# A ring of eight PSUM banks for the seven products, sums on VectorE, and four weight sets converted during the attention

## The chip, the cores and the metric

The kernel runs on one core of a Trainium2 chip. The metric is device time in microseconds (us); for the kernel before it is 731.38 us, the median of three runs (730.93 to 731.45).

## The reference

Attention with a learned relative-position bias, then a layer that takes the maximum of three products:

```python
scores = (q @ k.transpose(0, 1, 3, 2)) / sqrt(64) + bias      # 4 batches, 8 heads, 576 x 576
attn = exp(scores - max); attn = attn / (sum(attn) + 1e-9)
x = (attn @ v).transpose(0, 2, 1, 3).reshape(2304, 512)
h = maximum(maximum(x @ w1, x @ w2), x @ w3)                  # w1, w2, w3: 512 x 768
out = h @ w_out                                               # 768 x 512
```

All of it is float32. The four weight matrices arrive as 8-byte numbers and are turned into float32 by bit operations on the chip.

## The kernel before, in words

The program has four stages. Instructions go to each engine in the order in which the code is written; every engine works its own list in that order, so an instruction that waits holds up all behind it.

1. Bias stage (to about 60 us): VectorE, ScalarE and TensorE make the position bias.
2. Attention (to about 311 us): 80 steps of scores, exponential, normalisation (GpSimd), transposes and the product with v. `step` (L363) writes one step; its argument `more` is a list of generators, each of which is advanced once in the step. One is `first()`: it converts weights. `convert` (L469) loads half a set (512 KB) and makes five VectorE passes (L479, L481, L484, L487, L492) over 512 columns; two such halves are a weight set. In the attention sets 0 and 1 and the six pieces of `w_out` are converted. Another generator, `combine(0)`, makes the operands of the first third of the tokens.
3. Product stage (311 to 643 us): x @ w1, x @ w2, x @ w3 as 9 weight sets (`s`: three matrices for three pairs of hidden blocks) times three token thirds (`x`), 27 groups in all, set after set. A group (`group`, L584) forms a 2 x 2 block product with seven block products p1 to p7 in place of eight; their sums give four results c11, c12, c21, c22, which are kept as maxima in `ht`. One product is six matmuls of 384 columns, since each operand is a high and a low part (hi*h, hi*l, lo*h, over two halves). p1 and p6 share one PSUM tile `p16` of two banks, p5 and p7 another, `p57`; ScalarE copies p1, p5 and p2 to SBUF (L599, L605, L614), VectorE adds four products to SBUF tiles, and GpSimd makes three sums of 384 columns. Between the products the generator `work(s)` is advanced: `load_w` converts set s + 1, `split_w` forms its seven weight combinations (four GpSimd sums `ws`) and splits them into high (`wh`, ScalarE) and low parts (`wl`, GpSimd, 768 and 1024 columns). During set 0 `combine(x + 1)` is advanced instead.
4. Second product (646 to 727 us): `h` went to DRAM (`store`), comes back transposed in blocks (`load_h`, `hin`), is split (`hh`, `hl`) and multiplied with the split `w_out`.

DMAs are issued from one queue (SP), in the order of the code.

Of the kernel before, what the change touches and what calls it, by code (L numbers as in the profile page):

```python
# [9 lines left out]
F32 = mybir.dt.float32  # L10
# [9 lines left out]
def kernel(  # L20
# [31 lines left out]

    def ps_t(name):
        return psums[-1].tile([128, 512], F32, tag="t", bufs=2, name=name)
# [7 lines left out]
    wo_d = dram.tile([DFF, DM], F32, name="wo_d")  # L62
    raws = []
# [124 lines left out]
    class Attention:  # L188
        def __init__(self, pool):
            self.pool = pool  # L190
            self.data = {}
            self.st = {}
            self.et = {}
            self.pvq = []
            self.done = []
            self.vl = [pool.tile([128, 2, D], F32, name=f"vl{x}", bufs=1) for x in range(2)]
            for x in self.vl:
                nc.gpsimd.memset(x, 0.0)
            bias_t.extend(pool.tile([128, 2, S], F32, name=f"bias{t}", bufs=1) for t in range(NTQ))
            bias_t.append(pool.tile([128, S], F32, name="biasm", bufs=1))  # L200
# [268 lines left out]
    def convert(pool, srcs, out, name):  # L469
# [4 lines left out]
        for _ in range(2):  # L474
# [21 lines left out]
    wf = {}  # L496

    def load_w(wpool, s):
        fp, i = divmod(s, 3)
        m = (mw1, mw2, mw3)[i]  # L500
        raw = wpool.tile([128, 1024], F32, tag="wr", bufs=2, name=f"wr{s}")
        wf[s] = raw
        for d in range(2):
# [4 lines left out]
    def split_w(pool, wpool, s):  # L508
# [3 lines left out]
        hi = pool.tile([128, 1792], F32R, tag=f"wh{s % 2}", bufs=1, name=f"wh{s}")  # L512
        lo = pool.tile([128, 1792], F32R, tag=f"wl{s % 2}", bufs=1, name=f"wl{s}")
        wf[s] = (hi, lo)
        g = nc.gpsimd
        arith(g, q(sr, 0), q(raw, 0), q(raw, 2), ALU.add)
        nc.scalar.copy(hi[:, 0:768], raw[:, 256:1024])
# [5 lines left out]
        yield  # L523
        nc.scalar.copy(hi[:, 768:1792], sr)
        arith(g, lo[:, 0:768], raw[:, 256:1024], hi[:, 0:768])
        yield
        arith(g, lo[:, 768:1792], sr, hi[:, 768:1792])
# [5 lines left out]
    def moe(pool, wpool, xa, xb):  # L533
        ht = pool.tile([128, 2, NT], F32, name="ht", bufs=1)
        hv = ht.rearrange("p b (t n) -> p (b t) n", t=2)
# [5 lines left out]
        def load_wo(fs):  # L541
            raw = wpool.tile([128, 1024], F32, tag="wr", bufs=2, name=f"wor{fs[0]}")
            n = len(fs)
            nc.sync.dma_start(out=raw[:, 0:512 * n].rearrange("p (c o) -> p c o", c=n),
                              in_=wo_d[128 * fs[0]:128 * fs[-1] + 128].rearrange("(c p) o -> p c o", p=128))
            if fs[0] % 3 == 0:
                hi, lo = (pool.tile([128, 1536], F32R, tag=f"w{k}{'o' if fs[0] else 1}", bufs=1, name=f"wo{k}{fs[0]}")
                          for k in "hl")
                for x in range(3):
                    wo[fs[0] + x] = (hi[:, 512 * x:512 * x + 512], lo[:, 512 * x:512 * x + 512])  # L550
            for _ in range(3):
                yield
            for x, f in enumerate(fs):
                hi, lo = wo[f]
                src = raw[:, 512 * x:512 * x + 512]
                nc.scalar.copy(hi, src)
                arith(nc.gpsimd, lo, src, hi)
                yield
# [25 lines left out]
        def group(s, x, work):  # L584
            fp, i = divmod(s, 3)
            r = slice(TW * x, TW * x + TW)
            p16, p57 = ps_s(f"p16_{s}_{x}"), ps_s(f"p57_{s}_{x}")
            p1, p6, p5, p7 = (p[:, n, 0:TW] for p in (p16, p57) for n in range(2))
            p2, p4 = (ps_t(f"p{n}_{s}_{x}")[:, 0:TW] for n in (2, 4))
            p3 = psums[-1].tile([128, TW], F32, tag="pv" if x % 2 else "l", bufs=1, name=f"p3_{s}_{x}")  # L590
            m1, m2, m3, mu = (pool.tile([128, TW], F32, tag="m", bufs=4, name=f"m{n}_{s}_{x}") for n in "123u")
            if i:
                mm, mn = (pool.tile([128, 2, TW], F32, tag="mm", bufs=2, name=f"m{n}_{s}_{x}") for n in "mn")
                c21, c22, c11, c12 = (m[:, n] for m in (mm, mn) for n in range(2))
            else:
                c21, c22, c11, c12 = (hv[:, n, r] for n in range(4))
            v, g = nc.vector, nc.gpsimd
            product("p1", p1, s, x)
            nc.scalar.copy(m1, p1)  # L599
            next(work, None)  # L600
            product("p6", p6, s, x)
            arith(v, m2, p6, m1, ALU.add)
            next(work, None)
            product("p5", p5, s, x)
            nc.scalar.copy(mu, p5)  # L605
            next(work, None)
            product("p7", p7, s, x)
            arith(v, m3, p7, m2, ALU.add)
            arith(g, m2, m2, mu, ALU.add)
            arith(g, c22, m3, mu, ALU.add)  # L610
            next(work, None)
# [200 lines left out]
```

## Time and profile before

| | us |
|---|---|
| median of three runs | 731.38 |
| profiled execution | 729.17 |
| its span | 727.4 |
| TensorE busy | 620.4 (85%) |
| VectorE / GpSimd / ScalarE busy | 440.0 / 365.4 / 344.6 |

The profile is of one execution. Its span is what the engines' records cover; the execution's own time is 1.8 us longer. TensorE's busy share is high in all stages but means little by itself: matmuls are pipelined and their ends are modelled. What counts is the distance between the starts of matmuls, and the waits before them.

### The profile page before, as it was taken

Reading aid. Unit: us, or ns where it says so; the run is one execution under the profiler, and the core shown is the slowest. Engines: PE = TensorE matmul, PEld = TensorE weight load, DVE = VectorE, ACT = ScalarE, POOL = GpSimd, SP = SyncE. Lnnn points to the kernel's source line nnn. Section 1 sums busy time; section 2 is a strip of 40 time slices with the busy share of each in tenths; the row PEclk is TensorE's granted clock in tenths of the full one; section 3 lists DMA queues with packets and bytes.
Section 4 is the critical chain, followed back from the end, with each engine's and each line's share of the span. In section 5 each row is a group of like instructions: output and inputs, shape, how many; then the busy total and the mean of one; then the engine's idle time right before and its main releaser. Section 6 shows DMA issues by size and latency. Waiting matters only on the chain.

```text
span 727.4 us, 12064 instructions
## 1 busy us (share of the span) xinstructions
PE 620.4 (85%) x4342; PEld 486.3 (67%) x4342; DVE 440.0 (60%) x899; ACT 344.6 (47%) x794; POOL 365.4 (50%) x339
## 2 busy tenths in 40 slices
PE   8999999999999999977849495858676776879998
PEld 4457777666767667656748484747666765758887
DVE  7986778678868877878365625272825173632221
ACT  8988878887977887644121211111111112222232
POOL 3408666966665664568754525453544447610000
PEclk9999999999999999986999879897979697989999
DMA  6994462245337311110010321010222001365331
GB/s 179 276 341 156 119 192 91 83 146 154 117 98 221 119 60 27 52 43 1 0 59 0 116 72 59 0 59 0 79 81 86 1 29 45 96 210 187 136 126 70
DMA packets 59595, 72.50 MB, mean 100 GB/s; under 512 B 22800, under 2 KB 41616, under 8 KB 59536
## 3 DMA queue, kind: packets, MB, share of 16 engines
q1 hardware_dynamic: 59392, 71.44, 31.0%
q8 instruction: 34, 0.56, 0.3%
q10 hardware_dynamic: 144, 0.29, 0.1%
q14 instruction: 25, 0.20, 0.1%
HBM read 47.46 MB, written 24.26 MB: 99 GB/s over the span
## 4 chain that ended last, share of the span: by engine, by line
PE 63%; POOL 12%; DVE 8%; issue 6%; ACT 6%; DMA 4%; SPq 1%; DVEq 0%; ACTq 0%; POOLq 0%
PE pv L343 11%; PE s L250 10%; PE tp L304 10%; PE p L580 6%; PE p L582 5%; PE p L581 5%; PE o L686 4%; PE o L687 4%; PE o L689 3%; POOL ws L413 3%; DMA w<-in_moe_w_dram 3%; PE bp L134 3%; POOL m L413 2%; DVE m L413 1%; POOL ht L413 1%
## 5 line engine op out<-in xcount | busy, mean ns | idle before, releaser
L285 POOL TENSOR_SCALAR e<-e,rc 128x576 f32<-128x576 f32 x144 | 106.4, 754 | 72.8 <-DVE rc L282 39.9
L272 ACT ACTIVATE e<-sn,nm 128x576 f32<-128x576 f32 x144 | 110.9, 772 | 42.0 <-DVE nm L260 40.2
L260 DVE CUSTOM_DVE_ANT_0 sn<-s,bias 128x576 f32<-128x576 f32 x128 | 91.7, 754 | 41.1 <-PE s L250 39.5
L413 POOL TENSOR_TENSOR m<-m,mu 128x384 f32<-128x384 f32 x27 | 30.9, 1146 | 141.2 <-DVE m L413 141.2
L413 DVE TENSOR_TENSOR m<-p,m 128x384 f32<-128x384 f32 x54 | 29.9, 554 | 102.9 <-PE p L582 98.1
L304 PEld LDWEIGHTS tp<-ident,e 128*128 128x128 f32 x576 | 61.4, 141 | 34.7 <-issue 24.0
L580 PE MATMUL p<-t2h,wh 128*128 128x384 f32 x54 | 25.0, 462 | 69.5 <-ACT m L599 69.5
L304 PE MATMUL tp<-ident,e 128*128 128x128 f32 x576 | 80.8, 280 | 0.9 <-ACT et L399 0.8
L343 PE MATMUL pv<-et,vt 128*64 128x256 f32 (+1 forms) x496 | 73.6, 417 | 0.5 <-DVE xb L359 0.5
L580 PEld LDWEIGHTS p<-t2h,wh 128*128 128x128 f32 x54 | 12.3, 228 | 78.4 <-ACT m L599 78.4
L219 POOL TENSOR_TENSOR kl<-kr,kh 128x640 fp32r<-128x640 f32 x16 | 35.6, 2222 | 47.5 <-ACT kh L218 47.5
L250 PE MATMUL s<-kh,qh 64*128 64x288 f32 (+1 forms) x288 | 57.2, 343 | 1.3 <-ACT bs L154 0.9
L402 DVE COPY et<-tp 128x512 f32<-128x512 f32 x64 | 43.7, 683 | 12.9 <-PE tp L304 12.8
L413 DVE TENSOR_TENSOR hl<-hin,hh 128x768 fp32r<-128x768 f32 x18 | 17.1, 957 | 56.4 <-ACT hh L570 56.4
L605 ACT COPY mu<-p 128x384 f32<-128x384 f32 x27 | 12.9, 479 | 75.9 <-PE p L582 75.9
L250 PE MATMUL s<-kl,qh 64*128 64x288 f32 (+1 forms) x288 | 48.6, 293 | 0.0
L686 PE MATMUL o<-woh,hh 128*128 128x512 f32 (+1 forms) x114 | 44.5, 395 | 4.4 <-ACT hh L570 4.4
L250 PE MATMUL s<-kh,ql 64*128 64x288 f32 (+1 forms) x288 | 48.0, 290 | 0.0
L399 ACT COPY et<-tp 128x512 f32<-128x512 f32 x80 | 45.9, 573 | 3.4 <-PE tp L304 3.4
L343 PEld LDWEIGHTS pv<-et,vt 128*64 128x64 f32 x496 | 30.4, 136 | 22.7 <-issue 8.2
L687 PE MATMUL o<-wol,hh 128*128 128x512 f32 (+1 forms) x114 | 44.6, 396 | 0.0
L134 PE MATMUL bp<-hid,w2s 128*32 128x79 f32 (+51 forms) x640 | 41.0, 391 | 2.2 <-DVE hid L113 1.7
(145 smaller groups left out, 1635.1 us busy)
## 6 DMA issues: line engine op xcount, KB each, us to landing
bias_d<-bs SPq DMA_DIRECT2D x36, 295.5 KB, 5.1
bias<-bias_d SPq DMA_DIRECT2D x16, 576.0 KB, 4.8
w<-in_moe_w_dram SPq DMA_DIRECT2D x36, 256.0 KB, 3.1
h_d<-ht SPq DMA_DIRECT2D x18, 384.0 KB, 3.1
hin<-h_d SPq DMA_DIRECT2D x6, 1152.0 KB, 5.7
qr<-in_qd_dram SPq DMA_DIRECT2D x16, 320.0 KB, 3.7
kr<-in_kd_dram SPq DMA_DIRECT2D x16, 320.0 KB, 4.3
out_dram<-ot SPq DMA_DIRECT2D x17, 256.0 KB, 2.0
```

Of the source, the lines that this page charges most:

```text
L134: nc.tensor.matmul(bp[32 * c:32 * c + 32, o:o + w], lhsT=w2s, rhs=src, start=True, stop=True)
L250: nc.tensor.matmul(ss[h][:, x, 0:HALF], lhsT=u[q][p, r], rhs=u[k][p, c:c + HALF], start=(j == 0), stop=(j == 2))
L260: nc.vector.tensor_tensor_reduce(out=sn.rearrange("p (a b) -> p a b", a=2), in0=st["s"][h][:, :, 0:HALF], in1=bt.rearrange("p (a b) -> p a ...
L272: nc.scalar.activation(st["e"][:, S * h:S * h + S], sn, ACTF.Exp, scale=-1.0, bias=nm, accum_out=st["sm"][:, h:h + 1])
L285: nc.gpsimd.tensor_scalar(out=e, in0=e, scalar1=rc[:, h:h + 1], scalar2=1.0, op0=ALU.mult, op1=ALU.mult)
L304: nc.tensor.transpose(tp[:, 128 * c:128 * c + 128], e2[:, k0:k0 + 128], ident)
L343: nc.tensor.matmul(pv[p], lhsT=w, rhs=x, start=(c == 0), stop=(c == NTQ))
L399: nc.scalar.copy(*tps[0])
L413: eng.tensor_tensor(out=out, in0=f(a), in1=f(b), op=op)
L580: nc.tensor.matmul(o, lhsT=hi[:, r], rhs=h[:, j], start=(j == 0), stop=False)
L686: nc.tensor.matmul(po, lhsT=hh[:, f], rhs=woh[:, r], start=(f == 0), stop=False)
L687: nc.tensor.matmul(po, lhsT=hh[:, f], rhs=wol[:, r], start=False, stop=False)
```

## The change

In the product stage each of the seven products gets a bank of its own from one ring of eight (`bank`), in a PSUM pool that replaces the attention's. Only p1 and p5 are copied by ScalarE; VectorE adds p6, p7, p2, p4 and p3 straight from their banks, and GpSimd makes one sum of 768 columns per group. The order of the products is p1, p5, p6, p7, p2, p4, p3. Sets 0 and 1 run interleaved by token third (0,0), (1,0), (0,1), ...; sets 2 to 8 as before.

The first of the five conversion passes goes to ScalarE (absolute value, times 2^16), which leaves four on VectorE. Sets 3, 2, 0 and 1 are converted in the attention; 3 and 2 are parked in DRAM (`w_d`) and loaded back. `first()` is advanced a second time in two of five steps, and `combine(0)` starts two steps earlier. `split_w` is cut in two: `sum_w` (GpSimd) follows the conversion, and `split_w` of set s runs in the first group of set s - 1. `w_out` is split piece by piece in the last set, and the last third's `store` stands ahead of the first `load_h`.

```diff
+    def bank(name):
+        return psums[-1].tile([128, 512], F32, tag="p", bufs=8, name=name)
...
-        nc.vector.tensor_scalar(out=t, in0=high, scalar1=0x7FFFFFFF, scalar2=None, op0=ALU.bitwise_and)
-        yield
-        nc.vector.tensor_scalar(out=a, in0=t.bitcast(F32), scalar1=2.0 ** -15, scalar2=2.0 ** 16,
-                                op0=ALU.max, op1=ALU.mult)
+        nc.scalar.activation(a, high.bitcast(F32), ACTF.Abs, scale=2.0 ** 16)
+        yield
+        nc.vector.tensor_scalar(out=a, in0=a, scalar1=2.0, scalar2=None, op0=ALU.max)
...
+    def raw_w(wpool, s, parked=False):
...
+        if parked:
+            nc.sync.dma_start(out=raw, in_=w_d[s])
+            return
...
+    def sum_w(wpool, s):
...
+        arith(g, q(sr, 0), q(raw, 0), q(raw, 2), ALU.add)
+        yield
+        arith(g, q(sr, 1), q(sr, 0), q(raw, 1))
+        yield
+        arith(g, q(sr, 2), q(raw, 1), q(raw, 0))
+        yield
+        arith(g, q(sr, 3), q(raw, 3), q(sr, 1))
+        yield
+
+    def split_w(pool, s):
...
         nc.scalar.copy(hi[:, 0:768], raw[:, 256:1024])
+        arith(nc.gpsimd, lo[:, 0:768], raw[:, 256:1024], hi[:, 0:768])
         yield
         nc.scalar.copy(hi[:, 768:1792], sr)
+        arith(nc.gpsimd, lo[:, 768:1792], sr, hi[:, 768:1792])
         yield
...
+            nc.scalar.copy(m1, made("p1"))
+            next(work, None)
+            nc.scalar.copy(m5, made("p5"))
+            next(work, None)
+            arith(v, mp[:, 1], made("p6"), m1, ALU.add)
+            next(work, None)
+            arith(v, mp[:, 0], made("p7"), mp[:, 1], ALU.add)
+            both = bass.AP(tensor=m5.tensor, offset=m5.offset, ap=[list(m5.ap[0]), [0, 2], [1, TW]])
+            g.tensor_tensor(out=q[:, 1:3], in0=mp, in1=both, op=ALU.add)
+            next(work, None)
+            arith(v, c11, made("p2"), m1, ALU.add)
+            next(work, None)
+            arith(v, c21, made("p4"), mp[:, 0], ALU.add)
             if i:
+                arith(v, acc[:, 0:2], acc[:, 0:2], q[:, 0:2], ALU.max)
             next(work, None)
+            arith(v, c12, made("p3"), u, ALU.add)
             if i:
+                arith(v, acc[:, 3:5], acc[:, 3:5], q[:, 3:5], ALU.max)
...
+        order = [(s, x) for x in range(NX) for s in (0, 1)] + [(s, x) for s in range(2, NSET) for x in range(NX)]
+
+        def weights():
+            yield from raw_w(wpool, 2, True)
+            yield from sum_w(wpool, 2)
+            for s in range(2, NSET):
+                while done[0] < (5 if s == 2 else 3 * s - 3):
+                    yield
+                yield from split_w(wpool if s % 2 == 0 else pool, s)
+                if s + 1 < NSET:
+                    yield from raw_w(wpool, s + 1, s + 1 < PARK)
+                    yield from sum_w(wpool, s + 1)
...
+            for s in range(PARK - 1, 1, -1):
+                yield from raw_w(wpool, s)
+                nc.sync.dma_start(out=w_d[s], in_=wf[s])
+            yield from raw_w(wpool, 0)
+            yield from sum_w(wpool, 0)
+            yield from split_w(wpool, 0)
...
-        store(KFF // 2 - 1, NX - 1)
...
+            if n >= 2 * NS and n % NS in (0, 4) and n < NSTEP:
+                more.append(w0)
+            if 9 * NS - 2 <= n < 9 * NS + 1 or n >= NSTEP - 2:
```

GpSimd's list where set 4 gives way to set 5, before (`m2`, `mm`, `mn`: sums of a group, named by set and token third; `ws5`, `wl5`: weights of set 5):

```order
L413 TENSOR_TENSOR m2_4_1_6074<-m2_4_1_6074,mu_4_1_6076 128x384
L413 TENSOR_TENSOR mm_4_1_6077<-m3_4_1_6075,mu_4_1_6076 128x384
L413 TENSOR_TENSOR mn_4_1_6078<-mn_4_1_6078,m1_4_1_6073 128x384
L413 TENSOR_TENSOR ws5_6124<-wr5_6007 128x256
L413 TENSOR_TENSOR ws5_6124<-ws5_6124,wr5_6007 128x256
L413 TENSOR_TENSOR ws5_6124<-wr5_6007 128x256
L413 TENSOR_TENSOR ws5_6124<-wr5_6007,ws5_6124 128x256
L413 TENSOR_TENSOR wl5_6126<-wr5_6007,wh5_6125 128x768
L413 TENSOR_TENSOR wl5_6126<-ws5_6124,wh5_6125 128x1024
```

and now (`q`: the one sum of a group):

```order
L417 TENSOR_TENSOR ws5_5970<-wr5_5829,ws5_5970 128x256
L417 TENSOR_TENSOR wl5_6021<-wr5_5829,wh5_6020 128x768
L417 TENSOR_TENSOR wl5_6021<-ws5_5970,wh5_6020 128x1024
L620 TENSOR_TENSOR q4_0_6008<-mp4_0_6011,m5_4_0_6010 128x768
L620 TENSOR_TENSOR q4_1_6086<-mp4_1_6089,m5_4_1_6088 128x768
```

The weights of set 5 stood behind the second group of set 4; now their sums are made in set 3, and the split stands ahead of the sum of set 4's first group.

GpSimd's list at the start of the product stage, before (`t1l_1`, `b11l_1`: low parts of the second token third's operands):

```order
L413 TENSOR_TENSOR b22l_0_5035<-xb22_0_909,b22h_0_5003 128x768
L413 TENSOR_TENSOR t1l_1_5082<-t1_1_5064,t1h_1_5073 128x768
L413 TENSOR_TENSOR m2_0_0_5054<-m2_0_0_5054,mu_0_0_5056 128x384
L413 TENSOR_TENSOR ht_5047<-m3_0_0_5055,mu_0_0_5056 128x384
L413 TENSOR_TENSOR b11l_1_5097<-xb11_1_911,b11h_1_5084 128x768
```

and now:

```order
L417 TENSOR_TENSOR ws1_5085<-wr1_4671,ws1_5085 128x256
L417 TENSOR_TENSOR wl1_5102<-wr1_4671,wh1_5101 128x768
L417 TENSOR_TENSOR wl1_5102<-ws1_5085,wh1_5101 128x1024
L417 TENSOR_TENSOR ws2_5123<-wr2_5121 128x256
L417 TENSOR_TENSOR ws2_5123<-ws2_5123,wr2_5121 128x256
L417 TENSOR_TENSOR t1l_1_5144<-t1_1_5119,t1h_1_5133 128x768
L417 TENSOR_TENSOR ws2_5123<-wr2_5121 128x256
L620 TENSOR_TENSOR ht_5107<-mp0_0_5110,m5_0_0_5109 128x768
L417 TENSOR_TENSOR b11l_1_5160<-xb11_1_912,b11h_1_5146 128x768
```

The weights of set 1 and the sums of set 2 have come in ahead of the first group's sum and of the next third's operands; `wr2` is the parked set, which is loaded into the buffer that `wl1` reads.

The SP queue at the end of the product stage, before (`h_d<-ht`: the stores; `hin`: the transposed loads):

```order
L544 DMA wor2_6960<-wo_d_62 128x512
L632 DMA h_d_61<-ht_5047 256x1x384 x4
L563 DMA hin0_7118<-h_d_61 128x6x384
L563 DMA hin1_7120<-h_d_61 128x6x384
L632 DMA h_d_61<-ht_5047 256x1x384 x2
```

and now:

```order
L554 DMA wor4_7041<-wo_d_62 128x512
L554 DMA wor5_7082<-wo_d_62 128x512
L636 DMA h_d_61<-ht_5107 256x1x384 x2
L577 DMA hin0_7094<-h_d_61 128x6x384
L577 DMA hin1_7096<-h_d_61 128x6x384
```

The last two stores, which need the last maxima, now stand ahead of the first load.

## Rows read from the trace of the kernel before

**Rows 1.** Stages: PE, PEld, DVE, ACT, POOL busy; clock, DMA share, GB/s.

```profile
60.00:311.00 251.00, 248.79 (x2136) 173.39 (x2133) 196.80 (x517) 202.08 (x549) 160.83 (x179) 1.00 0.39 117
311.00:643.00 332.00, 238.19 (x1136) 217.46 (x1134) 174.47 (x229) 66.86 (x117) 183.70 (x143) 0.86 0.15 48
643.00:646.30 3.30, 0.01 (x1) 0.01 (x1) 1.79 (x4) 0.89 (x2) 0.00 (x0) 0.73 1.07 386
646.30:727.40 81.10, 78.01 (x342) 63.37 (x342) 17.11 (x18) 23.13 (x36) 0.00 (x0) 0.96 0.38 133
```

**Rows 2.** TensorE's waits, product stage: total us, times, longest.

```profile
PE p L580 <- ACT m L599: 69.5, 27, 8.4
PE p L580 <- ACT mu L605: 16.8, 27, 1.9
```

**Rows 3.** TensorE in order of time, product stage: start, us, instruction, wait before.

```profile
392.04 0.44 PE L580 MATMUL p<-t2h,wh 128*128 128x384 f32 x1 [0.65 <-ACT m L599]
...
395.27 0.34 PE L581 MATMUL p<-t3l,wh 128*128 128x384 f32 x1
...
400.13 0.33 PE L582 MATMUL p<-b11h,wl 128*128 128x384 f32 x1
401.11 0.45 PE L580 MATMUL p<-t2h,wh 128*128 128x384 f32 x1 [0.65 <-ACT m L599]
...
417.62 0.69 PE L580 MATMUL p<-t2h,wh 128*128 128x384 f32 x1 [8.10 <-ACT m L599]
```

**Rows 4.** VectorE by shape, 345 to 640 us: count, busy, mean ns, idle.

```profile
L413 DVE TENSOR_TENSOR m<-p,m 128x384 f32<-128x384 f32 x50 | 27.7, 554 | 98.2 <-PE p L582 98.1
L413 DVE TENSOR_TENSOR ht<-ht,mm 128x768 f32<-128x768 f32 x17 | 25.4, 1495 | 4.0 <-POOL mm L413 2.8
L413 DVE TENSOR_TENSOR ht<-ht,mn 128x768 f32<-128x768 f32 x17 | 18.4, 1084 | 3.7 <-POOL mn L413 2.1
L492 DVE SCALAR_TENSOR_TENSOR wr<-w,signm,wt 128x512 uint32<-128x512 uint32 x14 | 15.4, 1101 | 0.3
L487 DVE SCALAR_TENSOR_TENSOR wt<-w,wt 128x512 uint32<-128x512 uint32 x14 | 14.4, 1029 | 0.2
L484 DVE TENSOR_SCALAR wt<-wa 128x512 uint32<-128x512 uint32 x14 | 10.8, 774 | 0.5
...
L481 DVE TENSOR_SCALAR wa<-wt 128x512 f32<-128x512 f32 x14 | 5.8, 417 | 0.0
```

**Rows 5.** GpSimd by shape, 345 to 640 us.

```profile
L413 POOL TENSOR_TENSOR m<-m,mu 128x384 f32<-128x384 f32 x25 | 27.6, 1105 | 139.7 <-DVE m L413 139.7
...
L413 POOL TENSOR_TENSOR wl<-ws,wh 128x1024 fp32r<-128x1024 f32 x8 | 18.9, 2368 | 0.0
L413 POOL TENSOR_TENSOR ws<-wr 128x256 f32<-128x256 f32 x16 | 15.1, 946 | 0.0
L413 POOL TENSOR_TENSOR wl<-wr,wh 128x768 fp32r<-128x768 f32 x8 | 14.4, 1804 | 0.0
```

**Rows 6.** GpSimd and VectorE in order of time, operand sums of 768 columns.

```profile
299.56 0.95 DVE L413 TENSOR_TENSOR t<-xb,xb 128x768 f32<-128x768 f32 x1
...
321.11 2.52 POOL L413 TENSOR_TENSOR b11l<-xb,b11h 128x768 fp32r<-128x768 f32 x1
...
322.01 2.44 DVE L413 TENSOR_TENSOR t<-xb,t 128x768 f32<-128x768 f32 x1
```

**Rows 7.** A ScalarE pass over 512 SBUF columns; a 512 KB load.

```profile
L556 ACT CAST woh<-wor 128x512 fp32r<-128x512 f32 x6 | 3.5, 621 | 2.8 <-DMA wor<-wo_d 2.8
...
w64o<-in_moe_w_out_dram SPq DMA_DIRECT2D x6, 512.0 KB, 4.1
```

**Rows 8.** The chain of waits ahead of the second product.

```profile
639.86 5.53 DMA hin<-h_d
645.41 0.84 ACT hh L570
```

**Rows 9.** The SP queue in order of time: the issue of two loads.

```profile
639.86 0.95 SPq L563 DMA_DIRECT2D hin<-h_d  x2
```

More of the change, by code (lines that the diff above doesn't have):

```diff
@@ L603, in group @@
[L603 to L611, printed above, removed]
-            next(work, None)
-            product("p2", p2, s, x)
-            nc.scalar.copy(c11, p2)
-            arith(g, c11, c11, m1, ALU.add)
-            next(work, None)
@@ L617, in group @@
[L617 to L626 removed]
+            acc = ht[:, x]
+            q = pool.tile([128, 5, TW], F32, tag="q", bufs=1, name=f"q{s}_{x}") if i else acc
@@ new lines, in group, with made @@
+            c21, c22, u, c11, c12 = (q[:, n] for n in range(5))
+            m1, m5 = (pool.tile([128, TW], F32, tag="m", bufs=3, name=f"m{n}_{s}_{x}") for n in "15")
+            mp = pool.tile([128, 2, TW], F32, tag="mp", bufs=2, name=f"mp{s}_{x}")
+            v, g = nc.vector, nc.gpsimd
+            def made(p):
+                o = bank(f"{p}_{s}_{x}")[:, 0:TW]
+                product(p, o, s, x)
+                return o
+            nc.scalar.copy(m1, made("p1"))
+            next(work, None)
@@ L648, in moe @@
-        late = []
-        for s in range(NSET):
-            w = work(s)
-            for x in range(NX):
-                more = combine(x + 1, xa, xb) if s == 0 and x + 1 < NX else w
-                group(s, x, more)
-                if more is not w:
-                    for _ in more:
-                        pass
-                if s % 3 == 2 and (s + 1 < NSET or x + 1 < NX):
-                    store(s // 3, x)
-            for _ in w:
-                pass
+        order = [(s, x) for x in range(NX) for s in (0, 1)] + [(s, x) for s in range(2, NSET) for x in range(NX)]
@@ new lines, in weights @@
+        def weights():
[8 more added lines that the diff above has]
+                    yield from sum_w(wpool, s + 1)
+            while done[0] < 24:
+                yield
+            for f in range(KFF // 2):
+                yield from load_wo(f)
+            while done[0] < 25:
+                yield
+            for f in range(KFF // 2, KFF):
+                yield from load_wo(f)
@@ new lines, in sums, with slots @@
+        def sums(x):
+            yield from combine(x, xa, xb)
+        done = [0]
+        late = []
+        sx = [sums(x) for x in range(1, NX)]
+        ww = weights()
+        def slots(n):
+            while True:
+                if n < 2 * NX - 2:
+                    next(sx[n // 2], None)
+                next(ww, None)
+                yield
+        for n, (s, x) in enumerate(order):
+            done[0] = n
+            if n < 2 * NX and n % 2 == 0 and n:
+                for _ in sx[n // 2 - 1]:
+                    pass
+            group(s, x, slots(n))
+            if s % 3 == 2:
+                store(s // 3, x)
@@ L661, in moe @@
+        for _ in ww:
+            pass
         xb.release()
@@ L754 @@
         apool.release()
+        psums.pop().release()
+        psums.append(ctx.enter_context(tc.tile_pool(name="psum_m", bufs=1, space=PSUM, reuse_waits="tile")))
         xb = tc.alloc_tile_pool(name="xb", bufs=1, side="right", reuse_waits="tile")
         with tc.tile_pool(name="moe_p", bufs=1, reuse_waits="tile") as mp:
+            for _ in split_w(mp, 1):
+                pass
             moe(mp, wpool, xa, xb)
```

104 lines of the change are left out of this document (33 added, 71 removed).

## The prediction

> **What bounds the kernel now.** I read the stretches of the four stages first, then TensorE's waits in the longest of them, then the order of time there, and last the durations of what the change adds. The reader is to see in the stretches that the attention leaves TensorE nothing to give (248.8 busy of 251 us, clock 1.00), while the product stage takes 332 us with TensorE 238 us busy at a mean granted clock of 0.86 [rows 1]. No other engine is full there either: GpSimd 184, VectorE 174, ScalarE 67 us. A stage in which nobody is full is bound by waits, and the list of waits names two: p6 waits for ScalarE's copy of p1 (27 times, 69.5 us) and p7 for the copy of p5 (27 times, 16.8 us) [rows 2]. Both pairs share a PSUM tile.
>
> The order of time gives the sizes [rows 3]. Between 395.27 and 400.13 there are 29 matmuls, so 28 distances: 4.86/28 = 0.1736 us each, or 42 x 0.1736 = 7.29 us for a group. A quiet group lasts 401.11 - 392.04 = 9.07 us, so the two waits cost 1.78 us with their restart. At seven of the set changes the first wait is 7 to 8.4 us in place of 0.65; the row at 417.62 shows one (8.10 us), and that its matmul then lasts 0.69 us in place of 0.45: after such a pause TensorE is at the lower of its clock's two levels, 1.2 GHz. There ScalarE's copy stands behind the cast of the weight sums `ws`, which GpSimd makes only after the sums of the group. So 332 us are 27 x 7.29 = 197 of matmuls, 27 x 1.78 = 48 of the two waits, about 52 to 55 of set changes (7 x 7.5), and some 33 left: the lower clock after those waits, and the first groups, where the operands of the next token third are late.
>
> **The change part by part.**
>
> *Waits removed.* With eight banks TensorE may run eight products ahead of the last one read, a group and one product, so neither copy is on its path. The weights of a set are split a whole set before their use, from sums made earlier still. That takes away the 48 and the 53 us, and the time at the lower clock. What is late next is one of three: TensorE itself (197 us), VectorE, or GpSimd.
>
> *VectorE per set.* A group costs five additions from PSUM, 5 x 0.554 = 2.77 us, and two maxima, 1.495 + 1.084 = 2.58 [rows 4]; three groups are 8.3 + 7.7 = 16.0. A set converted meanwhile costs 2 halves x (0.417 + 0.774 + 1.029 + 1.101) = 6.6 (I take the new pass for the like of the old L481) [rows 4]. That is 22.7 us against TensorE's 21.9. Sets 2, 4 and 5 have both; I add 2.5 for two waits in each (the second half's load, 4.1 us after the first half is done [rows 7], and the sum q behind both weight splits): 25.2, so 3 x 3.3 = 10 us over the floor. Sets 3 and 6 write their results without maxima, 15 us, and sets 7 and 8 convert nothing, 16 us: TensorE bounds these four.
>
> *GpSimd per set.* Three sums of 768 columns, which the trace doesn't show for this operation; the subtraction of the same shape takes 1.80 undisturbed [rows 5] and 2.52 beside VectorE [rows 6], three sums of 384 before cost 1.105 each [rows 5]. I take 2.1. With four `ws` (0.95) and the splits (1.80 + 2.37) [rows 5] a set is 6.3 + 3.8 + 4.2 = 14.3 us: under 21.9.
>
> *The first six groups.* Here GpSimd is late. Counted from the attention's end: set 1's last conversion pass ends at about 1.3, its sums at 5, `wl1` (768) at 6.8; only then may the parked set be loaded, 0.5 + 4.1, so at 11.4 [rows 7, 9], and GpSimd's list stands at its first `ws2` until that lands. From there: four `ws2` (3.8), the four low parts of the next third (1.8 + 3 x 2.5 = 9.3) and two sums (4.2), to 28.7; the second pair of groups without `ws2`, 13.5, to 42. TensorE, one group ahead, starts the fifth group near 38 to 44 and ends the sixth at about 53, against 6 x 7.29 = 43.7 without a wait: 9 us.
>
> So the product stage: 197 + 9 + 10 = 216 us, in place of 332. Bounds: 199 (all covered) and 245 (below).
>
> *The attention.* Fourteen half sets in place of ten: VectorE 14 x 4 = 56 passes for 50, ScalarE 14 new ones of 0.62 us [rows 7], 8.7 us in all, two more halves' loads for each parked set, the parking stores and a second advance of the generator. ScalarE is busy 202 of 251 us, VectorE 197 [rows 1], so the passes fit beside TensorE. The new ScalarE pass waits for its load, and behind it in ScalarE's list stand the copies that free TensorE's transpose banks. Seven advances in five steps are one half set; after set 0 its load is issued when the last half's last pass is done, one step (251/80 = 3.1 us) before the ScalarE pass, while issue and landing take 0.5 + 4.1 [rows 7]: some 1.9 us of wait in each of eight halves. ScalarE's slack per five steps (49/16 = 3.1 us of 15.7) covers 0.62 + 1.9. From both sides 0 and 8.7 + 15 = 24 us; I take 3, near the cover, since every transpose has a step of slack.
>
> *The end of the stage.* Before, the transposed load was issued at 639.86, some 3 us ahead of the stage's end, landed 5.53 later, and TensorE restarted after a pause of 3.3 us [rows 1, 8]. Now it stands on the SP queue behind two stores that need the last maxima: after TensorE's end an addition 0.55 and a maximum of 1 to 2, two issues of about 0.5 each [rows 9], then 5.5 and the cast of 0.84: 9.3 us. That is +6 (bounds +4 and +8). The second product, 81.1 us, keeps its instructions; its matmuls follow one another without a wait now, so eight banks in place of two change nothing.
>
> *The sum.* 311 + 3 + 216 + 9.3 + 81.1 = 620.4 us of span against 727.4. The profiled execution was 1.8 above its span, and the median of the runs is 2.2 above that: 624 us.
>
> **The rivals.**
>
> A. All is hidden: 311 + 199 + 7.3 + 81.1 + 4 = 602. For it: VectorE's means include times beside a busier GpSimd. Against: 22.7 is above 21.9 already.
>
> B. VectorE and GpSimd get in each other's way more than their means show. In the rows a VectorE sum that takes 0.95 alone took 2.44 when it began in a GpSimd sum, and ended 0.8 after it [rows 6]: it stood until GpSimd was done. All VectorE work on SBUF operands then adds to GpSimd's: 14.3 + 7.7 + 6.6 = 28.6, and with a third of the PSUM additions stuck behind, 31 us in sets 2, 4 and 5 (+18 over my 25.2), with some 11 more in the first groups, where both carry the most: 245, so 311 + 3 + 245 + 9.3 + 81.1 + 4 = 653. Against: VectorE's means hold such waits already. The Trainium skill (SBUF — State Buffer, "Who interferes with whom") says that where VectorE has two SBUF inputs and GpSimd reads SBUF, the second to issue "fully blocks until the first finishes". By that rule B is the case in every set; the row agrees for the one pair, and my sum by the means would be too low by up to the 29 us.
>
> C. ScalarE's new pass holds up the attention by its full 24 us: 645. Against: the slack just counted.
>
> D. The banks don't free TensorE, and a wait per group stays, 48 us: 672. Against: each product now is its own tile, and p5 follows p1 without needing its copy.
>
> E. Slower: VectorE and GpSimd work in turn throughout. VectorE's last addition and its maxima need GpSimd's sum, and that sum needs VectorE's p7; if the in-order lists let neither run ahead, sets 2, 4, 5 take 22.7 + 15.5 each (GpSimd with 2.52 per sum), 3 and 6 30, 7 and 8 30, the first six groups 48 + 51 = 99 (VectorE: 6 x 2.77, 3 x 2.58, 14 operand passes of about 1.7; GpSimd: 8 x 2.3, 6 x 2.1, 20 of weights): 335, so 311 + 3 + 335 + 9.3 + 81.1 + 4 = 743. It decides once the stage passes 323 us, 36 a set. Against: the bank ring lets VectorE stand a whole group behind TensorE, and GpSimd's weights depend on no group.
>
> **How the numbers follow.** Forecast 0.56, A 0.16, B 0.16, C 0.06, D 0.03, E 0.03. The range 601 to 655 takes in A, B and C and leaves out D, E and odd ends: about 0.85. About 0.2% is what a measurement of this kernel can tell from no change. Faster by more is all but E and a case between D and E: 0.96; within 0.2%: 0.01; slower: 0.03.
>
> **What would show it.** Right: matmuls of the product stage 0.174 us apart over whole groups with no wait for ScalarE; sets 3, 6, 7 and 8 at 22 us, 2, 4 and 5 at 25; the first six groups about 53, with GpSimd idle for the parked load early; a pause of about 9 us before the second product; an attention that ends at 311 to 316. Wrong: sets of 30 us with TensorE waiting for VectorE (B), waits of TensorE for ScalarE in the attention (C), or a wait for ScalarE in each group (D).

## The result: 634.75 us, 0.869 of the time before

The changed kernel takes 634.75 us (median of four runs, 633.36 to 636.11); the kernel before took 731.15 us on the same chip. The ratio is 0.8685, with a 95% interval of 0.8656 to 0.8714. The forecast was 624 us, with a range of 601 to 655. The profiled execution took 636.11 us, with a span of 634.1.

### The profile page after: what moved, and what is told of

Read it like the earlier page. It is cut to its first block, busy times and chain, and to the rows that moved or that the text cites. A ratio compares the mean times of both kernels' runs of the same rounds, so it can differ in the third digit from the quotient of the medians.

```text
span 634.1 us, 12010 instructions
## 1 busy us (share of the span) xinstructions
PE 592.1 (93%) x4342; PEld 471.1 (74%) x4342; DVE 425.1 (67%) x902; ACT 343.9 (54%) x791; POOL 326.5 (51%) x285
## 4 chain that ended last, share of the span: by engine, by line
PE 53%; DVE 10%; ACT 10%; POOL 9%; DMA 9%; issue 7%; SPq 1%; POOLq 0%; DVEq 0%; ACTq 0%
PE pv L347 10%; PE s L254 9%; PE tp L308 9%; PE o L710 4%; PE o L711 4%; PE o L713 4%; PE p L594 3%; PE p L595 3%; PE p L596 3%; DMA w<-in_moe_w_dram 3%; POOL q L620 3%; POOL wl L417 3%; DMA w64o<-in_moe_w_out_dram 2%; ACT bs L158 2%; DVE ht L417 2%
## 5 line engine op out<-in xcount | busy, mean ns | idle before, releaser
L289 POOL TENSOR_SCALAR e<-e,rc 128x576 f32<-128x576 f32 x144 | 108.8, 768 | 59.5 <-DVE rc L286 32.8
L308 PE MATMUL tp<-ident,e 128*128 128x128 f32 x576 | 83.0, 282 | 6.2 <-ACT et L403 5.6
L223 POOL TENSOR_TENSOR kl<-kr,kh 128x640 fp32r<-128x640 f32 x16 | 35.6, 2227 | 57.5 <-ACT kh L222 57.4
L417 DVE TENSOR_TENSOR ht<-ht,q 128x768 f32<-128x768 f32 x36 | 38.6, 1073 | 37.9 <-POOL q L620 37.3
L406 DVE COPY et<-tp 128x512 f32<-128x512 f32 x64 | 43.7, 682 | 22.3 <-PE tp L308 22.3
L620 POOL TENSOR_TENSOR q<-mp,m 128x768 f32<-128x768 f32 x18 | 33.3, 1848 | 35.8 <-DVE mp L417 35.8
L347 PEld LDWEIGHTS pv<-et,vt 128*64 128x64 f32 x496 | 30.5, 136 | 24.0 <-issue 10.5
L254 PEld LDWEIGHTS s<-kh,qh 64*128 64x128 f32 (+1 forms) x288 | 31.3, 184 | 13.2 <-issue 7.5
L714 ACT COPY ot<-o 128x512 f32<-128x512 f32 (+1 forms) x19 | 10.7, 564 | 55.7 <-PE o L713 55.7
L117 DVE TENSOR_SCALAR hid<-sm,bp 128x528 f32<-128x528 f32 (+17 forms) x108 | 40.7, 461 | 0.0
```

What stands on the lines that cost most here:

```text
L254: nc.tensor.matmul(ss[h][:, x, 0:HALF], lhsT=u[q][p, r], rhs=u[k][p, c:c + HALF], start=(j == 0), stop=(j == 2))
L289: nc.gpsimd.tensor_scalar(out=e, in0=e, scalar1=rc[:, h:h + 1], scalar2=1.0, op0=ALU.mult, op1=ALU.mult)
L308: nc.tensor.transpose(tp[:, 128 * c:128 * c + 128], e2[:, k0:k0 + 128], ident)
L347: nc.tensor.matmul(pv[p], lhsT=w, rhs=x, start=(c == 0), stop=(c == NTQ))
L406: nc.vector.tensor_copy(*tps[1])
L417: eng.tensor_tensor(out=out, in0=f(a), in1=f(b), op=op)
```

## The profile after

The stages come first, as in [rows 1]: stretch, its length, busy time of TensorE, weight load, VectorE, ScalarE and GpSimd, the clock, DMA share and GB/s. The product stage is cut behind its sixth group.

```profile
60.00:319.20 259.20, 251.47 (x2132) 173.83 (x2130) 203.02 (x524) 209.12 (x562) 164.44 (x179) 0.99 0.41 125
...
319.20:378.90 59.70, 48.97 (x252) 47.44 (x253) 45.16 (x49) 19.61 (x30) 43.83 (x25) 0.91 0.06 18
378.90:541.70 162.80, 157.82 (x883) 153.86 (x882) 107.05 (x176) 38.60 (x69) 93.53 (x62) 0.99 0.25 81
...
541.70:552.70 11.00, 0.01 (x1) 0.00 (x0) 2.81 (x4) 1.66 (x4) 3.71 (x2) 0.63 0.76 258
552.70:634.10 81.40, 78.37 (x342) 63.69 (x342) 17.12 (x18) 23.12 (x36) 0.00 (x0) 0.96 0.35 122
```

The attention became 8.2 us longer, the product stage 109.5 us shorter (332 to 222.5), the pause ahead of the second product 7.7 us longer, and the second product 0.3. That is 93.3 of the 93.3 us between the spans (727.4 and 634.1). Before, the last matmul of the product stage ends at 641.9, ahead of the cut at 643.0; cut there, as it is here, the product stage before is 330.9 us and the pause 4.4, so that the changes of these two are -108.4 and +6.6.

TensorE's waits in the product stage (total us, times, longest), to be held against [rows 2]:

```profile
PE p L594 <- DVE ht L417: 11.6, 6, 3.8
PE p L594 <- DVE q L417: 2.2, 3, 1.8
...
PE p L594 <- ACT m L612: 0.3, 1, 0.3
```

The 86.3 us of waits for ScalarE's copies are 0.3 us now. Nearly all the rest are waits for a bank that VectorE has not read yet. In order of time (start, us, instruction), a late group starts and ends without a wait:

```profile
519.68 0.34 PE L594 MATMUL p<-b11h,wh 128*128 128x384 f32 x1
...
526.97 0.33 PE L594 MATMUL p<-b11h,wh 128*128 128x384 f32 x1
```

A group is 7.29 us, the 42 matmuls at 0.1736 of [rows 3]. The sets 2 to 8 take 22.8, 24.2, 22.0, 26.8, 23.0, 21.9 and 22.0 us: 162.8, against 7 x 21.9 = 153.3 without a wait. (The distances between the starts of groups give these, here and in the experiments.)

VectorE by shape, 366 to 540 us (count; busy us, mean ns of one; idle us before it), and GpSimd's sum below, against [rows 4, 5]:

```profile
L417 DVE TENSOR_TENSOR ht<-ht,q 128x768 f32<-128x768 f32 x32 | 34.3, 1072 | 35.9 <-POOL q L620 35.4
...
L495 DVE SCALAR_TENSOR_TENSOR wr<-w,signm,wt 128x512 uint32<-128x512 uint32 x10 | 7.5, 752 | 0.3
L490 DVE SCALAR_TENSOR_TENSOR wt<-w,wt 128x512 uint32<-128x512 uint32 x10 | 6.9, 692 | 0.3
L485 DVE TENSOR_SCALAR wa<-wa 128x512 f32<-128x512 f32 x10 | 5.6, 556 | 13.6 <-ACT wa L483 13.6
L487 DVE TENSOR_SCALAR wt<-wa 128x512 uint32<-128x512 uint32 x10 | 4.2, 417 | 0.0
...
L620 POOL TENSOR_TENSOR q<-mp,m 128x768 f32<-128x768 f32 x17 | 31.4, 1849 | 35.8 <-DVE mp L417 35.8
```

VectorE's maxima and the last three conversion passes got shorter; the pass behind ScalarE's did not (0.556 us against 0.417 of the old L481), and GpSimd's splits kept their times. The 98 us in which VectorE waited for TensorE are nearly gone. In their place VectorE stands 35.4 us for GpSimd's sum `q`, and GpSimd 35.8 us for VectorE's `mp`, from which `q` is made.

The first groups in order of time, on GpSimd and VectorE (in brackets the wait before, and for what), against [rows 6]:

```profile
325.81 2.41 POOL L417 TENSOR_TENSOR wl<-ws,wh 128x1024 fp32r<-128x1024 f32 x1
329.54 0.74 POOL L417 TENSOR_TENSOR ws<-wr 128x256 f32<-128x256 f32 x1 [1.32 <-DMA wr<-w_d]
...
320.29 0.95 DVE L417 TENSOR_TENSOR t<-xb,xb 128x768 f32<-128x768 f32 x1
...
326.68 2.36 DVE L417 TENSOR_TENSOR t<-xb,xb 128x768 f32<-128x768 f32 x1
...
332.93 1.47 DVE L417 TENSOR_TENSOR t<-t,xb 128x768 f32<-128x768 f32 x1 [3.42 <-POOL t1l L417]
```

The same sum takes 0.95 us alone and 2.36 when it begins inside GpSimd's `wl`: `wl` ends at 328.22, the sum 0.82 later at 329.04. VectorE's fourteen operand passes of these six groups take 26.5 us, 1.9 each, and in 58.7 of the 59.7 us at least one of the two engines is busy. The lists are chained as well: the sum at 332.93 stood 3.42 us for GpSimd's `t1l`.

Behind the two longest waits of these groups TensorE is at the lower of its two levels (granted clock 0.50 from 360.2 to 367.0), and matmuls start some 0.32 us apart in place of 0.17:

```profile
361.88 0.66 PE L594 MATMUL p<-b11h,wh 128*128 128x384 f32 x1 [3.77 <-DVE ht L417]
...
362.65 0.52 PE L596 MATMUL p<-b11h,wl 128*128 128x384 f32 x1
362.98 0.52 PE L594 MATMUL p<-b11h,wh 128*128 128x384 f32 x1
```

There are 26 such matmuls in the six groups; they make 3.9 of the 15.4 us over 6 x 7.29 = 43.7.

The chain of waits ahead of the second product, against [rows 8]:

```profile
543.09 1.45 DVE ht L417
...
544.56 0.52 SPq L636
...
545.13 6.67 DMA hin<-h_d
...
551.82 0.84 ACT hh L584
...
552.70 0.79 PE o L710
```

## The experiments

Lines behind an edit have other numbers than in the changed kernel (L491 and L497 are its L490 and L495). "To before" is the ratio to the kernel before in the same session, with its 95% interval; the changed kernel stands at 0.8685. The cuts of the stages are those of each profiled execution.

**The ring alone.** The kernel before with nothing but the ring of banks:

```diff
-            p16, p57 = ps_s(f"p16_{s}_{x}"), ps_s(f"p57_{s}_{x}")
-            p1, p6, p5, p7 = (p[:, n, 0:TW] for p in (p16, p57) for n in range(2))
...
+            p1, p6, p5, p7, p2, p4, p3 = (bank(f"p{n}_{s}_{x}")[:, 0:TW] for n in (1, 6, 5, 7, 2, 4, 3))
```

> The kernel before with one edit: the seven products of a group (and the second product) take banks of one ring of eight; the order of products, the sums, the weights and the attention stay. Theory: the 48 us of the two waits per group and the 52 of the set changes are separate costs; the ring takes the first and leaves the second, 731 - 48 = 683 us (678 to 690), with waits of 7 to 9 us at seven set changes. Rival 1: the weights of the next set, which are made within the set, take the 36 us of a set by themselves; a faster TensorE only waits longer at each change (13 to 14 us) and the time stays at 715 to 731. Rival 2: banks alone carry the change: 650 or less.

680.18 us, 0.9295 to before (0.9256 to 0.9334). The product stage falls to 282.3 us, from 330.9 by the same cut. TensorE's waits there:

```profile
PE p L585 <- POOL wl L416: 32.8, 12, 4.3
PE p L584 <- POOL b11l L416: 9.7, 2, 6.2
```

The waits for the copies are gone with the shared tiles, and quiet groups stand at 7.29 us. What is left are the set changes, with 13 to 15 us for a group, and the late operands (`b11l`) of the first groups. So the ring brings some 49 us, and all that was changed besides the other 60 of the stage.

**The longer attention.** First, sets 2 and 3 not parked but converted in the product stage:

```diff
-    PARK = 4
+    PARK = 2
```

> The changed kernel, but only sets 0 and 1 are converted in the attention, sets 2 and 3 in the product stage like the rest. Theory: the product stage's first six groups, where VectorE and GpSimd are late already (59 us against 43.7 of matmuls), take two more conversions badly: 7 to 10 us longer; the attention gets 2 to 3 us back: 638 to 643 us. Rival: the conversions fit beside the matmuls there as in the later sets, and the attention's 8 us come back: 627 to 630.

637.56 us, 0.8706 to before (0.8677 to 0.8735): not to be told from the changed kernel. The attention ends at 315.6 (319.2), and the product stage takes 225.4 us (222.5): by these two profiles, what parking saves in one stage it costs in the other. The first six groups, for which I had expected 7 to 10 us more, are 2.6 us shorter (56.5), although VectorE converts a set there; set 1 was ready earlier, its last low part 2.1 us behind the attention's end in place of 9.0. Sets 2 to 8 are 5.7 us longer.

Then a load one step further ahead of its ScalarE pass:

```diff
-        for _ in range(2):
+        for _ in range(3):      # in the attention; 2 in the product stage
...
-            if n >= 2 * NS and n % NS in (0, 4) and n < NSTEP:
+            if n >= 2 * NS and n % NS in (0, 2, 4) and n < NSTEP:
```

> The changed kernel, but in the attention the ScalarE pass of a conversion comes one advance of the generator later after its load, and the generator is advanced a second time in three of five steps in place of two. Theory: the attention lost its 5 to 6 us (of 8) between 188 and 245 us to ScalarE standing at that pass until the load had landed; with a longer lead TensorE's waits for ScalarE's copies fall from 5.6 us to about 1 and the attention ends 4 to 6 us earlier: 629 to 631 us. Rival: it is the added work itself (14 passes of 0.67 us) that delays the copies: nothing changes, 634 to 636.

638.59 us, 0.8719 (0.8688 to 0.875); the attention ends at 321.6. TensorE's waits between 60 and 320 us:

```profile
PE pv L347 <- DVE xb L363: 4.1, 6, 0.9
...
PE tp L308 <- ACT et L403: 1.0, 2, 0.8
```

In the changed kernel the wait for `et` is 5.6 us; it fell, and waits for VectorE's `xb` took its place. ScalarE's waits for loads fell from 6.6 us to 0.2. But the edit also made a new wait, of VectorE for ScalarE's pass, which is 2.1 us in the changed kernel:

```profile
DVE wa L485 <- ACT wa L483: 11.2, 6, 1.9
```

So the attention did not get shorter when the load's wait went, as my theory had it; but the run exchanged one wait for another, and is no clean test of the theory.

Last, the first pass given back to VectorE:

```diff
-        nc.scalar.activation(a, high.bitcast(F32), ACTF.Abs, scale=2.0 ** 16)
+        nc.vector.tensor_scalar(out=t, in0=high, scalar1=0x7FFFFFFF, scalar2=None, op0=ALU.bitwise_and)
...
+        nc.vector.tensor_scalar(out=a, in0=t.bitcast(F32), scalar1=2.0 ** -15, scalar2=2.0 ** 16,
+                                op0=ALU.max, op1=ALU.mult)
```

> The changed kernel with five conversion passes on VectorE again, none on ScalarE. If ScalarE's wait for the load is what held the attention up, TensorE's waits for ScalarE's copies go (5.6 us to under 1.5), but VectorE now stands at the same loads with the scores' passes behind it: attention 2 to 5 us shorter, product stage 1 to 4 us longer for the fifth pass, 631 to 636 us in all. Rival: VectorE has no room for 14 more passes in the attention, which gets longer by 3 or more: 638 to 645.

652.36 us, 0.8897 (0.886 to 0.8935): 15.5 us more (the difference of the ratios, 0.0212, by 732). The attention ends at 325.7, the product stage takes 229.4. TensorE's first wait in the attention, and what VectorE waits for there:

```profile
PE pv L347 <- DVE xb L363: 12.4, 9, 2.5
...
DVE wto L483 <- DMA w64o<-in_moe_w_out_dram: 9.5, 5, 2.7
DVE wt L483 <- DMA w<-in_moe_w_dram: 4.5, 3, 2.9
```

The 24 passes are 0.43 us each at their shortest and 0.91 on average, 21.8 us; and VectorE now stands at the loads itself, 14.0 us in the attention. VectorE has no room there for both; the run does not tell the work from the waits.

**The first six groups.** They take 59.1 us. The sums of set 2, which wait for the parked load, not ahead of the fifth group:

```diff
             yield from raw_w(wpool, 2, True)
+            while done[0] < 4:
+                yield
             yield from sum_w(wpool, 2)
```

> The changed kernel, but GpSimd's sums of weight set 2 are held back until the fifth group of the product stage. Theory: GpSimd's list at the stage's start (its wait for the parked set, 1.3 us, and the four sums, 2.9 us) stands in the way of the next third's operands; without it the first two groups (20.2 us) lose 3 to 4 us and the first six fall from 59.1 to 55 to 56. Rival: the sums only move to the fifth and sixth group, where GpSimd also splits set 2, and the six groups keep their 59 us.

632.61 us, 0.863 (0.8616 to 0.8645); the six groups take 57.7 us. The load at the head of GpSimd's list costs 1 us or so, not the 3 to 4 expected: unchanged, these groups took 58.3 to 59.4 us in four other runs. The rest of the 4 us between the ratios is in stages that the edit doesn't touch. Then six low parts of the operands are left out, once those on VectorE (`t3`, `t2`, `t4` of the second and third token third), once those on GpSimd (`b11`, `b21`, `b22`):

```diff
+            if x and eng is v:                         # or: x and n in ("b11", "b21", "b22")
+                return h, h
```

> The changed kernel without the three low parts (t3, t2, t4) that VectorE makes for the second and third token thirds; the products read the high part in their place, so the number of matmuls is the same. Theory: in the first four groups VectorE and GpSimd take turns at SBUF operands, so a pair of groups lasts the sum of both engines' undisturbed work (8.5 + 11.0 = 19.5 us, measured 20.2 and 21.9); three passes of 0.95 less make each pair 2.5 to 3 us shorter, 5 to 6 us in all. Rival, as my prediction had it: GpSimd's own list sets the pace there; VectorE's passes count for nothing and the pairs lose 0 to 1 us each.

> The changed kernel without three low parts (b11, b21, b22) that GpSimd makes for the second and third token thirds; the products read the high part in their place. Theory (turns at SBUF operands): each pair of groups loses the undisturbed 3 x 1.82 = 5.5 us and comes to TensorE's own 14.6 to 16.5. Rival (GpSimd's list alone): it loses 3 x 2.5 = 7.5 us of GpSimd's time and comes to TensorE's 14.6. The two differ little here; together with the run without VectorE's low parts they tell whether one engine or both set the pace.

625.83 us, 0.854 (0.8523 to 0.8557), and 623.79 us, 0.8512 (0.8494 to 0.8531). The six groups of the two, first without VectorE's and then without GpSimd's (columns as in the stages above):

```profile
318.60:370.70 52.10, 46.73 (x252) 45.26 (x253) 33.19 (x42) 19.73 (x30) 41.83 (x25) 0.97 0.06 18
```

```profile
317.70:368.70 51.00, 46.17 (x253) 45.28 (x254) 37.62 (x48) 19.70 (x30) 29.60 (x19) 0.97 0.06 16
```

Either takes 7 to 8 us from the 59.1. Of each, 2.4 us are TensorE's clock: with shorter waits it is granted 0.97 in place of 0.91, and matmuls at the lower level cost 1.5 us in place of 3.9. Some 5 us are left, 0.8 to 0.95 per pass. If GpSimd alone were the bound, VectorE's passes would have brought nothing. In the changed kernel the two are busy 45.2 and 43.8 us in 59.7, and a pass that stands for the other engine's counts as busy. How much of the 5 us is such standing, and how much the chain through both lists (sum, high part, low part), these runs don't tell.

**The pause ahead of the second product.** The last store behind the first two loads, which don't need it:

```diff
-            if s % 3 == 2:
+            if s % 3 == 2 and n + 1 < len(order):
                 store(s // 3, x)
...
         split(0)
+        store(KFF // 2 - 1, NX - 1)
```

> The changed kernel, but the last third's store stands behind the first two transposed loads, as in the kernel before. Theory: the load is held by the two stores that wait for the last maxima; without them it is issued about 2 us before the last matmul as before, and TensorE's pause of 11.0 us ahead of the second product falls to 4 to 5: 6 us less in all (0.9%). Rival: the pause is set by the w_out splits, which GpSimd ends 4 us after the last matmul, or by the buffers of the loads, which the last products still read: 8 us or more stay.

626.71 us, 0.8553 (0.854 to 0.8565). The SP queue, then TensorE, in order of time:

```profile
536.48 0.96 SPq L577 DMA_DIRECT2D hin<-h_d  x2
538.85 2.46 SPq L636 DMA_DIRECT2D h_d<-ht  x2
...
543.80 0.80 PE L711 MATMUL o<-woh,hh 128*128 128x512 f32 x1 [5.78 <-ACT hh L584]
```

The pause is 5.8 us in place of 11.0. The profiled spans are 9.6 us apart (9.7 by the ratios): 5.2 is the pause, 2.7 an attention that ended earlier with the same instructions, and the rest (1.0 in the product stage, 0.7 in the second product) is in stages that the edit doesn't touch either. With the ring alone, where the loads stand ahead of the last store too, the pause is 7.6 us: earlier stores that wait for VectorE hold them until 0.5 us behind the last matmul. So what counts is all that stands ahead of the loads.

**The 9.5 us over the floor in sets 2 to 8.** First without the conversions of that stage:

```diff
-                    yield from raw_w(wpool, s + 1, s + 1 < PARK)
+                    yield from raw_w(wpool, s + 1, True)      # loads w_d[2 + (s + 1) % 2]
```

> Leaves out the conversion of sets 4 to 8 in the product stage: in their place the two parked sets are loaded again, with the same sums and splits, so that the later blocks of w1 to w3 are not used. In the changed kernel sets 2 to 8 take 162.8 us against 7 x 21.9 = 153.3, 9.5 over. Theory (the conversions' passes, with the waits that stand in VectorE's list, make the excess): sets 2 to 8 within 2 us of 153.3, the product stage about 213, the median about 626 (8 to 10 below the changed kernel). Rival (maxima and sums q of the groups make VectorE and GpSimd wait for each other, conversions or not): at least 6 of the 9.5 us stay and the median is 632 or more.

626.88 us, 0.8581 (0.8556 to 0.8606). Sets 3 to 8:

```profile
401.50:533.00 131.50, 131.45 (x758) 131.13 (x756) 73.60 (x115) 28.12 (x51) 76.24 (x50) 1.00 0.20 65
```

They are 131.5 us, 6 x 21.9, where the changed kernel has 140.0: without conversions the groups' own sums hold nothing up. Set 2 became worse (26.2 for 22.8), so the seven sets take 157.7 and not the 155 that the theory allowed. There GpSimd makes the parked set's sums and a split between the sums `q`; whether that is the reason stays open.

Are the conversions' waits to blame, or their work? The load four steps ahead:

```diff
-        for _ in range(2):
+        for _ in range(4 if fast else 2):      # fast: in the product stage
             yield
...
-        yield                                  # after two of VectorE's four passes
+        if not fast:
+            yield
```

> Changed kernel with four steps of the generator in place of two between the load of half a set and its ScalarE pass, in the product stage only; VectorE's four passes go out in pairs, so that a half takes one step less in all. Theory (the excess of 9.5 us in sets 2 to 8 is mostly VectorE standing in its list for ScalarE's pass, which waits for the load, 13.6 us in 10 halves): VectorE's wait for wa falls below 4 us, sets 2 to 8 to 154 to 157 us, the median to 628 to 630. Rival (it is VectorE's work, with GpSimd's beside it): the wait for wa falls, another takes its place, the sets stay at 161 or more and the median at 633 to 636.

632.83 us, 0.8648 (0.8624 to 0.8672); sets 2 to 8 161.7 us. VectorE's waits between 360 and 540 us, in the changed kernel and here:

```profile
DVE ht L417 <- POOL q L620: 35.4, 16, 5.5
DVE wa L485 <- ACT wa L483: 13.6, 7, 3.8
...
DVE ht L417 <- POOL ht L620: 3.3, 3, 1.1
```

```profile
DVE ht L417 <- POOL q L623: 35.4, 16, 5.5
DVE ht L417 <- POOL ht L623: 14.6, 7, 4.6
...
DVE wa L485 <- ACT wa L483: 1.2, 2, 0.7
```

The theory fell: 12.4 us of the wait for `wa` went, and 11.3 us came back as a longer wait for GpSimd's sum in sets 3 and 6 (there `q` is `ht` itself). All three remedies together:

> Three edits at once on the changed kernel: the last store behind the loads of the second product (alone ratio .855 to before, -9 to -10 us to the changed kernel), the sums of set 2 not before the fifth group (alone -4), and the load four steps ahead of its pass. If they add up: 622 without a gain of the third, 615 to 617 with the theory's gain of it. Rival (the sums of set 2 that come later push set 2's split into set 2's first group, and the third brings nothing): 624 to 627.

627.93 us, 0.8587 (0.8566 to 0.8608), nothing beyond the store alone: a first group pair 1 us shorter, sets of 161.7 us and a pause of 5.0, but an attention and a second product each longer than in the run with the store alone, by 2.3 and 0.9. The gains did not add up, neither to the 622 expected nor to the rival's 624 to 627; these differences are as large as the gains that were to be added.

Last, one edit on that kernel. The maxima and the last addition of a group go behind the next group's p6:

```diff
+            rest()                             # maxima and c12 of the group before
             arith(v, mp[:, 0], made("p7"), mp[:, 1], ALU.add)
...
-            if i:
-                arith(v, acc[:, 0:2], acc[:, 0:2], q[:, 0:2], ALU.max)
             next(work, None)
-            arith(v, c12, made("p3"), u, ALU.add)
-            if i:
-                arith(v, acc[:, 3:5], acc[:, 3:5], q[:, 3:5], ALU.max)
+            due.append((made("p3"), acc, q, s, x))
```

> One edit on the run before (store behind the loads, later sums, earlier load; 627.9 us, sets 2 to 8 161.7 us, VectorE 50 us in waits for GpSimd's sum q between 360 and 540 us): the two maxima of a group and its last addition stand in VectorE's list behind the next group's p6, so that they no longer wait right behind the sum q that they need. Theory (VectorE has 19.5 us of work in a set of 21.9, and the excess is its standing for q in its list): the wait for q falls below 15 us, sets 2 to 8 to 154 to 157 us, the first six groups to 54 to 57 from 58.0, the median to 618 to 622. Rival (VectorE's and GpSimd's work on SBUF operands, in turns, is what fills the sets): the passes get longer or another wait takes the place, sets 2 to 8 at 160 or more, the median at 626 to 629.

624.13 us, 0.8538 (0.8512 to 0.8565), the fastest with all work in it, level with the store alone within the intervals. Sets 2 to 8 fall from 161.7 to 158.4 us, the first six groups from 58.0 to 56.3. VectorE's wait for `q` fell from 35.6 us to 4.1, but its passes got longer (by shape, 360 to 540 us):

```profile
L417 DVE TENSOR_TENSOR ht<-ht,q 128x768 f32<-128x768 f32 x34 | 37.7, 1110 | 4.7 <-POOL q L624 4.1
L487 DVE TENSOR_SCALAR wt<-wa 128x512 uint32<-128x512 uint32 x10 | 14.7, 1467 | 0.3
L491 DVE SCALAR_TENSOR_TENSOR wt<-w,wt 128x512 uint32<-128x512 uint32 x10 | 14.6, 1455 | 0.3
```

One of them in order of time, beside GpSimd, and the next half's without:

```profile
407.45 2.60 POOL L417 TENSOR_TENSOR wl<-ws,wh 128x1024 fp32r<-128x1024 f32 x1
...
407.83 2.51 DVE L487 TENSOR_SCALAR wt<-wa 128x512 uint32<-128x512 uint32 x1
...
418.21 0.43 DVE L487 TENSOR_SCALAR wt<-wa 128x512 uint32<-128x512 uint32 x1
```

The theory got 3.3 of the 5 to 8 us that it expected in these sets. Of the 31.5 us that the wait lost, 18.0 came back as longer passes, (1467 - 428) + (1455 - 693) ns ten times each, and 8.5 as a longer wait for ScalarE's pass (1.4 to 9.9 us). The like wait for `ht` in sets 3 and 6 went too (14.5 to 0.7 us), and VectorE now waits 18.2 us for TensorE's p6 (1.1 before): on the whole it has room. But in five of the ten halves the two passes meet GpSimd and take 2.5 and 2.2 us in a row, and TensorE's only waits in these sets are four for VectorE's `mp`, 3.0 us. So both theories hold a part: VectorE's standing for `q` costs, and in half of the halves turns with GpSimd take its place.

The median missed the 618 to 622 expected by 2 us, and the pause took back 4.0: it is 9.0 us in place of 5.0. A store that waits for the moved maxima now stands on the SP queue ahead of the loads. They go out 1.1 us behind the last matmul; in the run before it was 1.5 us ahead of it:

```profile
529.79 2.99 SPq L649 DMA_DIRECT2D h_d<-ht  x2
...
533.55 1.33 SPq L580 DMA_DIRECT2D hin<-h_d  x2
```

## Why the prediction was right, and where its sizes were off

The mechanism was right, and the forecast 10.8 us low. By terms, of the span (620.4 foretold, 634.1 measured): attention +5.2, product stage +6.5, pause +1.7, second product +0.3.

- *Waits removed.* Right: the waits for copies went from 86.3 to 0.3 us, and the set changes with them. The ring alone brings 49 us, close to the 48 that I had put on the two waits.
- *The attention, +8.2 and not +3.* The mis-sized term. I took the work as hidden by slack counted over five steps. (The wait of 1.9 us per half in that count should read 4.6 - 3.1 = 1.5; measured, ScalarE waits for these loads six times, 6.6 us in all.) ScalarE's wait for a load does reach TensorE, as in these rows (ScalarE twice, TensorE):

```profile
242.13 0.68 ACT L483 ACTIVATE wao<-w64o 128x512 f32<-128x512 f32 x1 [1.66 <-DMA w64o<-in_moe_w_out_dram]
...
243.32 0.58 ACT L403 COPY et<-tp 128x512 f32<-128x512 f32 x1
...
244.04 0.63 PE L308 MATMUL tp<-ident,e 128*128 128x128 f32 x4 [1.28 <-ACT et L403]
```

  TensorE's waits in the attention grew from 2.0 to 7.5 us. Over the nine kernels whose attention has the same instructions its end lies between 316.4 and 321.4 us, the middle at 318.0, so some 7 us are the change's and the rest is spread. Whether the added passes cost them or the waits that come with them stays open: without the load's wait the attention was no shorter, but another wait had come in, and the 3.6 us that it lost with two sets less to convert lie within the spread.
- *The first six groups, 59.1 and not 53.* The step that failed in kind: I had GpSimd's list alone as the bound, and no time at the lower clock, which is 3.9 of the 6 us. The list's beginning came as foretold (the parked load is in 10.4 us behind the attention's end, foretold 11.4), yet either engine's low parts are worth some 5 us besides the clock. The two hold each other up; the row pair 325.81 and 326.68 shows a turn, the wait at 332.93 a link of the chain.
- *Sets 2 to 8: 162.8 for 163, by errors that cancel.* VectorE's work is less than foretold, 4.8 us for a converted set (2 x (0.556 + 0.417 + 0.692 + 0.752)) in place of 6.6, and 19.5 with the groups in place of 22.7. The waits are larger than the 2.5 us that I added. The excess lies in sets 3 and 5 most, not in 2, 4 and 5; I take it that the ring hands a delay on by up to a group and one product, but no run separates this. That conversions make it is shown by their removal (sets 3 to 8 at 21.9); that it is not one wait, by the two edits that each traded one wait for another.
- *The pause, 11.0 and not 9.3.* The chain is the one foretold. The load took 6.67 us in place of 5.53; in the other runs 5.6 to 7.2, and no run shows why. The 3.3 us that I read as the pause before were cut behind the stage's last matmul: it was 4.4, and the loads were issued 2 us ahead of the stage's end, not 3.
- *Rival B* was at work, as a part: in 378.9 to 541.7 VectorE is busy 107.1 us and GpSimd 93.5, together 200.6 of 162.8. By their timelines both are busy at once for 45 us only, and at least one of them in 155 of the 162.8; how much of this is turns and how much the loop through `q` isn't shown. In the first groups, where passes of either engine count, it goes furthest. The Trainium skill (SBUF — State Buffer, "Who interferes with whom") also names the one-operand `tensor_scalar` among the operations that can take the ports which VectorE shares with GpSimd. The rows of the last run agree: that pass takes 0.43 us alone and 2.51 beside `wl`. But that the wait falls on every set, as B had it, is refuted by sets of 22 us.
- *Rivals A, D and E* did not come: no set of 36 us, no wait per group. *C* came in small: its sign is there, TensorE's waits for ScalarE's copies in the attention (5.6 us, 1.5 before), but all that was added costs the attention some 7 us and not 24.

## What to carry to other kernels

Where two engines make a loop within a group (VectorE's sum, GpSimd's sum of it, VectorE's maximum of that), put the last step behind the next group's first, and expect only a part of the wait back: passes that had run alone then meet the other engine. Price what two engines cost each other by leaving out the work on each side once; if both help, neither list alone is the bound, and the granted clock tells how much of the gain is TensorE's clock. And look at what a queue does in order at a stage's end: a load that needs nothing new does not belong behind a store of the last result.

## What was not expected of the hardware

- VectorE's conversion passes became shorter without being touched (L484 0.774 to L487 0.417, L487 1.029 to L490 0.692 us), because their place in the list behind `q` keeps them from running beside GpSimd: of the ten passes of each line none did. Moved forward, five of ten did, and they took 1.467 and 1.455 on average.
- The end of the attention differs by up to 5 us between executions of the same instructions, so a stage's gain of 2 to 3 us can't be read from one profile.
- The second product takes the longer, the longer TensorE stays at the lower level (granted clock 0.50) after its start, and that does not follow the length of the pause before it. Behind a pause of 10.5 us (sums of set 2 later) it is there for 3.0 us and the second product takes 80.3; behind 5.8 (the store alone) 4.0 and 80.7; behind 11.0 (the changed kernel) 5.5 and 81.4; behind 5.0 (all three remedies) 6.2 and 81.6.
